# A list scheduler lays 600 plans, with a lag for TensorE's results, a rate for GpSimd beside VectorE, and one tile for two score banks

## The chip, the core and the metric

The kernel runs on one core of a Trainium2 chip. The metric is the device time of one execution in microseconds (us), the median of several runs. Besides, one execution is recorded by the hardware profiler; its span runs from the first to the last instruction of the core. The engines are called PE (TensorE's matmuls), PEld (its weight loads), DVE (VectorE), ACT (ScalarE), POOL (GpSimd) and SP (the queue that issues most DMAs). L918 is line 918 of the kernel before.

## What is computed

An attention with a block-causal mask (4 batches, 8 heads, 576 positions, head size 64) is followed by two MLPs over its 2304 tokens (512 to 2048 to 512), all in float32:

```python
scores = scale * q @ k.T                  # 8 heads, 4 batches, S = 576, D = 64
mask = pos[:, None] // 64 >= pos[None, :] // 64
attn = softmax(where(mask, scores, -1e9)) # exp, divided by sum + 1e-9
x = (attn @ v)                            # as (2304, 512)
r = maximum(x @ w_in, 0)                  # MLP 1
x = (s * (r * r) + b) @ w_out
h = x @ w2_in                             # MLP 2
return maximum(0.01 * h, h) @ w2_out
```

## The kernel before

**Tiles and stages.** Queries go in five blocks of 128 (the last of 64) positions, in the order 0, 1, 2, 4, 3 (`ORDER`). Block k sees 128 (k + 1) keys, the last one 576. MLP 1 of a block (`m_in`, `m_out`) runs while the attention of the next block is computed (`later_block`). MLP 1 has 16 hidden chunks f; each takes 4 chunks of three 512-column matmuls for h (L918; fp32r, split in a high and a low part, three products) and 4 times three for y (L961). ScalarE and VectorE make g, gh and gl from h between the two (L930 to L940). In the first block the weights of MLP 1 are decoded from pairs of words as they arrive (`first_weights`, `decode`, L345 to L371); from block 1 on the weights of MLP 2 are prepared and stored as `unit` (L461 to L495). After the last block, MLP 2 runs from 600 us on as seven products in place of eight over 384 columns (`in_pair`, L1174, and `out_phase`, L1239, with additions in L1154 and splits in L1046 and L1232).

**One attention unit** is a pair of heads of a batch. There are 16 for each block. The queries and keys are split (L712 to L716), TensorE writes the scores to the two banks `s` (L585 for blocks 0 and 1, L790 for the "flat" blocks 2 and 3, with two row groups in the array, L830 for block 4 with two halves of 288 keys), VectorE masks and takes the maximum (L796, L797, L834, L838), ScalarE the exponential with its sum (L800, L841), VectorE the reciprocal (L807, L848). Then p is normalised on GpSimd or VectorE (L577, L809, L849), TensorE transposes p by four 128-column pieces (L600) into bank `t`, ScalarE or VectorE takes that out as `pv` (L516, L518), and TensorE multiplies by v (L869).

**What sets the order.** All of this is put as steps into `Graph` by `G.add`: the engines that may do it with a cost on each, the steps whose result it needs (`after`), the buffers it opens and uses, a due time, whether it uses the port that VectorE and GpSimd share (`port`), the bytes of a DMA, the kind of TensorE work (`mode`: "f" for full matmuls, "r" for row-split scores, "c" for column-split products with v), and `behind`, steps that only must have been started before. `order` is an event-driven list scheduler: at each time every idle engine takes the ready step with the lowest due time whose buffers have room. On TensorE a change of mode counts as 10 times its `TURN` in due time. A result is there `LAT` = 0.04 us after a step's planned end. Of two steps with `port`, on VectorE and on GpSimd, one excludes the other. The steps are then issued in that order, each engine runs its own list in order, and real semaphores keep every dependency. In the plan, fillers (L622, dummy matmuls on `warm`) stand where TensorE has nothing else in the first 30 us.

The costs which the text uses: `act(n)` = 0.2 + n / 1200 us and 0.14 more with a sum, `dve(n)` = 0.155 + n / 960, `pool(n)` = 0.28 + 0.00085 n, a transpose 0.109, a chunk of three matmuls of T columns 3 (T / 2400 + 0.013).

## Time and profile before

| | us |
|---|---|
| median of 3 runs | 953.37 (953.12 to 954.3) |
| the profiled execution, device time | 956.59 |
| its span | 954.8 |
| TensorE's mean granted clock | 0.998 of full speed |

| engine | busy us | share | instructions |
|---|---|---|---|
| PE | 935.8 | 98% | 5780 |
| PEld | 828.2 | 87% | 5780 |
| DVE | 659.0 | 69% | 1321 |
| ACT | 564.7 | 59% | 1198 |
| POOL | 103.5 | 11% | 224 |

Busy is the time in which at least one instruction of the engine runs. A matmul's end is modelled and successive matmuls overlap, so TensorE's busy time tells where the engine had nothing at all, and not how fast it ran. Idle time is listed by the instruction that ended it and by what that one had waited for (the releaser).

### The profile page before, as it was taken

To read this page: it belongs to the slowest core of one execution; us is meant where nothing else is said; L and a number is where in the kernel's file an instruction comes from. 1 tells how busy PE (TensorE), PEld (TensorE's weight loads), DVE (VectorE), ACT (ScalarE), POOL (GpSimd) and SP (SyncE) were. 2 spreads that over 40 slices of the span, in tenths; PEclk is the share of its full clock that TensorE was granted. 3 is DMA by queue.
4 is the path that set the end of the run, shared out by engine and by line. 5 is a ranking of instruction groups with operands and counts; after the bars stand their busy time and mean duration, and the time that the engine had idled before them with its cause. 6 is when DMAs were issued, how large, how long until landed. Compare 5 with 4: busy or idle time off the path is not lost.

```text
span 954.8 us, 16614 instructions
## 1 busy us (share of the span) xinstructions
PE 935.8 (98%) x5780; PEld 828.2 (87%) x5780; DVE 659.0 (69%) x1321; ACT 564.7 (59%) x1198; POOL 103.5 (11%) x224
## 2 busy tenths in 40 slices
PE   9999999999999999999999999999999999999998
PEld 8677887777777888888878888899999999999998
DVE  5988878777587867766768664555595655855557
ACT  4766767675576656656558444454565646555443
POOL 1122221112121121122320000000000000000000
PEclk9999999999999999999999999999999999999999
DMA  8995487886748898587337981998229852147402
GB/s 235 341 303 184 130 290 222 287 308 181 231 136 262 262 303 260 153 251 233 110 94 236 383 284 60 372 417 363 98 61 330 309 183 100 50 181 292 162 1 67
DMA packets 147668, 208.27 MB, mean 218 GB/s; under 512 B 23552, under 2 KB 118400, under 8 KB 140928
## 3 DMA queue, kind: packets, MB, share of 16 engines
q1 hardware_dynamic: 145136, 206.42, 65.2%
q10 hardware_dynamic: 2448, 0.79, 0.4%
q8 instruction: 46, 0.75, 0.3%
q14 instruction: 38, 0.31, 0.1%
HBM read 154.47 MB, written 52.69 MB: 217 GB/s over the span
## 4 chain that ended last, share of the span: by engine, by line
PE 81%; DVE 6%; DMA 5%; ACT 2%; issue 2%; POOL 1%; SPq 1%; POOLq 0%; DVEq 0%; ACTq 0%
PE h L918 17%; PE y L961 16%; PE A L1239 10%; PE A L1174 10%; PE C L1174 5%; PE C L1239 5%; PE t L600 4%; PE o L869 4%; PE B L1239 3%; PE B L1174 2%; PE s L790 2%; PE s L585 1%; PE s L830 1%; PE warm L622 1%; DMA q<-in_q_dram 1%
## 5 line engine op out<-in xcount | busy, mean ns | idle before, releaser
L918 PE MATMUL h<-xh,w 128*128 128x512 f32 (+1 forms) x640 | 230.2, 389 | 2.2 <-DVE g L932 1.2
L961 PE MATMUL y<-gh,w 128*128 128x512 f32 (+1 forms) x640 | 185.8, 374 | 0.9 <-ACT yo L516 0.9
L918 PEld LDWEIGHTS h<-xh,w 128*128 128x128 f32 x640 | 119.2, 190 | 29.7 <-issue 4.1
L961 PEld LDWEIGHTS y<-gh,w 128*128 128x128 f32 x640 | 114.3, 188 | 21.2 <-ACT yo L516 1.2
L1232 ACT ACTIVATE gh<-G 128x384 fp32r<-128x384 f32 x168 | 86.9, 525 | 57.0 <-PE A L1239 21.6
L918 PE MATMUL h<-xl,w 128*128 128x512 f32 (+1 forms) x320 | 118.9, 372 | 0.7 <-DVE xl L698 0.7
L961 PE MATMUL y<-gl,w 128*128 128x512 f32 (+1 forms) x320 | 118.4, 370 | 0.0
L1174 PE MATMUL A<-xh,wi 128*128 128x384 f32 x384 | 112.9, 337 | 1.0 <-DVE G L1154 0.9
L1046 DVE TENSOR_TENSOR gl<-G,gh 128x384 fp32r<-128x384 f32 x168 | 91.4, 554 | 30.4 <-ACT gh L1232 28.7
L1239 PE MATMUL A<-gh,wo 128*128 128x384 f32 x384 | 98.0, 336 | 1.4 <-DVE Y L1154 1.4
L934 ACT ACTIVATE g<-h 128x512 f32<-128x512 f32 (+1 forms) x80 | 44.2, 553 | 84.1 <-PE h L918 77.2
L600 PE MATMUL t<-id_sb,p 128*128 128x128 f32 x400 | 67.5, 280 | 6.6 <-POOL p L577 3.1
L1174 PEld LDWEIGHTS A<-xh,wi 128*128 128x128 f32 x384 | 70.6, 188 | 2.9 <-DVE G L1154 1.5
L1239 PEld LDWEIGHTS A<-gh,wo 128*128 128x128 f32 x384 | 69.1, 188 | 2.4 <-DVE Y L1154 2.3
L961 PEld LDWEIGHTS y<-gl,w 128*128 128x128 f32 x320 | 60.3, 188 | 10.9 <-DVE gl L937 0.5
L600 PEld LDWEIGHTS t<-id_sb,p 128*128 128x128 f32 x400 | 46.8, 141 | 26.0 <-POOL p L577 5.9
L918 PEld LDWEIGHTS h<-xl,w 128*128 128x128 f32 x320 | 60.9, 190 | 8.2 <-DVE xl L698 1.0
L1188 ACT ACTIVATE G<-G 128x384 f32<-128x384 f32 x72 | 37.6, 524 | 47.2 <-DVE G L1154 47.2
L937 DVE TENSOR_TENSOR gl<-g,gh 128x512 fp32r<-128x512 f32 (+1 forms) x80 | 50.8, 635 | 20.1 <-ACT gh L936 16.5
L1174 PE MATMUL A<-xl,wi 128*128 128x384 f32 x192 | 64.5, 336 | 0.0
L1239 PE MATMUL A<-gl,wo 128*128 128x384 f32 x192 | 64.2, 335 | 0.0
L1046 DVE TENSOR_TENSOR G<-G 128x384 f32<-128x384 f32 x96 | 53.2, 555 | 12.8 <-ACT G L1188 11.2
(125 smaller groups left out, 1834.5 us busy)
## 6 DMA issues: line engine op xcount, KB each, us to landing
wi<-u_in SPq DMA_DIRECT2D x32, 896.0 KB, 7.8
wo<-u_out SPq DMA_DIRECT2D x28, 1024.0 KB, 9.0
w<-kept SPq DMA_DIRECT2D x16, 1024.0 KB, 7.9
u_in<-unit SPq DMA_DIRECT2D x16, 896.0 KB, 5.9
u_out<-unit SPq DMA_DIRECT2D x32, 448.0 KB, 4.6
early<-in_moe_w_in_dram SPq DMA_DIRECT2D x16, 512.0 KB, 5.9
early<-in_moe_w_out_dram SPq DMA_DIRECT2D x16, 512.0 KB, 6.4
kept<-w SPq DMA_DIRECT2D x8, 1024.0 KB, 7.7
```

The costliest lines, as they stand in the source:

```text
L600: e.transpose(tb()[:, x * 128:(x + 1) * 128], P()[:, pc:pc + 128], id_sb)
L790: e.matmul(out=o[h][:, :nk], lhsT=qs()[r, qc], rhs=kk()[r, :nk], start=(n == 0), stop=(n == 2))
L869: e.matmul(out=o()[64 * h:64 * h + 64, n * x:n * x + n], lhsT=V()[:, j, 64 * h:64 * h + 64], rhs=r, start=(j == 0), stop=(j == nj - 1),)
L918: e.matmul(out=h()[:, :T], lhsT=w()[:, wi, c * 128:(c + 1) * 128], rhs=x[blk, c]()[:, :T], start=(c == 0 and n == 0), stop=(c == KD - 1 an ...
L934: a = G.add({"ACT": act(T)}, lambda e: e.activation(out=g()[:, :T], in_=h()[:, :T], func=ACTF.Relu), [prev], [g], [h], due)
L937: lo = G.add({"DVE": dve(T)}, lambda e: e.tensor_tensor(out=gl()[:, :T], in0=g()[:, :T], in1=gh()[:, :T].bitcast(F32), op=ALU.subtract), [ ...
L961: e.matmul(out=y()[:, :W], lhsT=w()[:, wi, d * 128:(d + 1) * 128], rhs=x()[:, :W], start=(pos == 0 and n == 0), stop=(pos == NF - 1 and n ...
L1046: e.tensor_tensor(out=out, in0=x, in1=y, op=ALU.subtract)
L1174: e.matmul(out=x()[:, :NH], lhsT=in_w[n, i, c]()[:, s, ai], rhs=y()[:, c], start=(first and c == 0 and m == 0), stop=(c == 1 and m == 2), ...
L1188: {"ACT": act(NH)}, lambda e, y=y: e.activation(out=y(), in_=y(), func=ACTF.Lrelu), [a], [], [y], d2 + 2)
L1232: hi = G.add({"ACT": act(NH)}, lambda e, gh=gh, x=x: e.activation(out=gh(), in_=x(), func=ACTF.Copy), [a], [gh], [x], due - 2)
L1239: e.matmul(out=z[d]()[:, :NH], lhsT=out_w[n, r]()[:, 2 * i + d, s], rhs=y(), start=(first and i == 0 and m == 0), stop=(i == 3 and m == 2) ...
```

## The change

`order` becomes a search around the scheduler, which is now called `plan`. It lays the plan once with the due times as written, and then 599 times with some of them moved: it draws a stretch of 5, 15, 40 or 100 us of the best plan so far, moves the due times of 30% of the steps in it by up to 1.5 us either way, and for steps that may run on two engines sometimes fixes one. A plan that ends no later than the best becomes the best. The random numbers have a fixed seed. In `plan`:

- A result of TensorE is there `DRAIN` later (0.14, 0.25 or 0.32 us by mode).
- Steps with `port` on VectorE and GpSimd no longer exclude each other. While a VectorE step with `port` runs, a GpSimd step proceeds at 1 − `HELD` = 40% of its rate; VectorE is not slowed.
- Chunks of one sum on TensorE, and the parts of one unit's scores, are chained by `behind` in place of `after`; the products with v and the four parts of a product in `out_phase` are chained too.
- Each buffer gets its slot from the plan (`slot`), in the order in which slots came free, in place of a count.
- The two score banks are one tile of [128, 2, 512]. In the flat blocks, one memset and one maximum cover both heads; the block of 576 keys has one step on TensorE for both halves, one maximum over both, one exponential with one sum, and no minimum and sum of two halves.
- The loads of v for block 1 stay free of a wait; the products with v of block 0 now count in `att_done`.

`EARLY` is not used. The diff, cut to its core:

```diff
+    PLANS = 600
+    DRAIN = {"f": 0.14, "r": 0.25, "c": 0.32}
+    HELD = 0.6
+    EARLY = 13.7
...
     def order(self):
+
+        kept = [(s.left, s.due, s.eng) for s in self.steps]
+        users = {b: b.users for s in self.steps for b in s.uses}
+        for i, s in enumerate(self.steps):
+            s.place = (s.due, i)
+        r = random.Random(1)
+        best, moved, at, out = None, [(0.0, None)] * len(kept), None, None
+        for _ in range(self.PLANS):
+            new = list(moved)
+            if best is not None:
+                a, w = r.uniform(0.0, best), r.choice((5, 15, 40, 100))
+                for i, x in enumerate(at):
+                    if a <= x < a + w and r.random() < 0.3:
+                        d, e = new[i]
+                        if len(kept[i][2]) > 1 and r.random() < 0.5:
+                            e = r.choice([None, *kept[i][2]])
+                        new[i] = d + r.uniform(-1.5, 1.5), e
+            for s, (left, due, eng), (d, e) in zip(self.steps, kept, new):
+                s.left, s.due, s.at = left, due + d, None
+                s.eng = eng if e is None else {e: eng[e]}
+            for b, u in users.items():
+                b.users = u
+            got = self.plan()
+            if best is None or got is not None and self.end <= best:
+                best, moved, at = self.end, new, [s.at for s in self.steps]
+                out = [(s, s.on, s.at, s.eng) for s in got], {b: b.slot for b in users}
+        for s, *x in out[0]:
+            s.on, s.at, s.eng = x
+        for b, x in out[1].items():
+            b.slot = x
+        self.end = best
+        return [x[0] for x in out[0]]
+
+    def plan(self):
...
-            turn[k].sort(key=lambda s: s.rank, reverse=True)
+            turn[k].sort(key=lambda s: s.place, reverse=True)
...
+                    room[s.key] += 1
+                    slots[s.key].append(s.slot)
...
-                    if port is s:
-                        port = None
+                elif what == "pool":
+                    if e == turn_no:
+                        idle["POOL"], busy = True, None
+                        heapq.heappush(events, (t + self.AGAIN["POOL"], n, "done", s, None))
+                        n += 1
...
+                    b.slot = slots[b.key].pop(0)
...
-                if s.port and e in ("DVE", "POOL"):
-                    port = s
...
+                if e in ("DVE", "POOL") and s.port:
+                    if e == "POOL":
+                        busy = [s, s.eng[e] - self.AGAIN[e], t]
+                    elif busy is not None:
+                        u = min(max(held, busy[2]), t)
+                        busy[1:] = busy[1] - (1 - self.HELD) * (u - busy[2]) - (t - u), t
+                    if e == "DVE":
+                        held = end
+                    if busy is not None:
+                        w = max(held - t, 0.0)
+                        left = busy[1]
+                        left = left / (1 - self.HELD) if left <= w * (1 - self.HELD) else left + w * self.HELD
+                        turn_no += 1
+                        heapq.heappush(events, (t + left, n, "pool", busy[0], turn_no))
+                        n += 1
+                    if e == "POOL":
+                        continue
...
+                if e == "PE":
+                    end += self.DRAIN[s.mode]
...
+        "h": (ps("ps_h", 1), 1), "s": (ps("ps_s", 1), 2), "t": (ps("ps_t", 1), 1),
...
+            x = b.slot * ptn if name == "pt" else npt * ptn + b.slot * vn
...
+        if key == "s":
+            b = Buf("s", lambda: s_both()[:, b.slot])
+            return b
...
+        a = G.add({"PE": 0.208 * 4}, av, [*tr, fv_ok, pads], [o], [pt, fv] + [spare] * (p > 1), due, mode="c", behind=att_done if att_done[0] else [])
+        att_done[0] = a
...
+            vl = [G.add({"SP": 0.65}, v_load, before if blk > 1 else [], fresh, [V4], due=due - 8, run=512, nbytes=512 * (nk // 128 * 128))]
...
-                            e.matmul(out=o[h][:, :nk], lhsT=qs()[r, qc], rhs=kk()[r, :nk], start=(n == 0), stop=(n == 2))
+                            e.matmul(out=s_both()[:, h, :nk], lhsT=qs()[r, qc], rhs=kk()[r, :nk], start=(n == 0), stop=(n == 2))
...
-                    mk = G.add({"DVE": 0.13}, lambda e, x=bk[h]: e.memset(x()[:64, nk - 64:nk], NEG), [sc], uses=[bk[h]], due=due - 4.5)
-                    mx.append(G.add({"DVE": dve(nk)}, lambda e, nm=nm, h=h, x=bk[h]: e.reduce_max(out=nm()[:, h:h + 1], in_=x()[:, :nk], axis=AX.X, negate=True),
-                                    [mk], [nm] * (h == 0), [nm, bk[h]], due=due - 4))
+                mk = G.add({"DVE": dve(128)}, lambda e: e.memset(s_both()[:64, :, nk - 64:nk], NEG), [sc], uses=bk, due=due - 4.5)
+                mx = [G.add({"DVE": dve(2 * nk)}, lambda e, nm=nm: e.reduce_max(out=nm()[:, 0:2], in_=s_both()[:, :, :nk], axis=AX.X, negate=True),
+                            [mk], [nm], [nm, *bk], due=due - 4)]
...
-                    sc.append(G.add({"PE": 3 * (half / 2400 + 0.013)}, fn, ok, [bk[j]], [kh, kl_, qs], due - 5))
+                            e.matmul(out=s_both()[:, j, :half], lhsT=qs()[:, qc, :128], rhs=kk()[:, half * j:half * j + half], start=(n == 0), stop=(n == 2))
+
+                sc = G.add({"PE": 6 * (half / 2400 + 0.013)}, fn, ok, bk, [qs, kh, kl_], due - 5)
...
-                neg = G.add({"DVE": 0.2}, lambda e, nm=nm: e.tensor_scalar(
-                    out=nm()[:, 0:1], in0=nm()[:, 0:1], scalar1=nm()[:, 1:2], scalar2=None, op0=ALU.min), mx, uses=[nm], due=due - 4)
-                ex = [
...
+                mx = G.add({"DVE": dve(nk)}, lambda e, nm=nm: e.reduce_max(out=nm()[:, 0:1], in_=s_both()[:, :, :half], axis=AX.XY, negate=True),
+                           [sc], [nm], [nm, *bk], due=due - 4)
+                ex = G.add({"ACT": act(nk, 1, True)}, lambda e, nm=nm, l=l, P=P: e.activation(
+                    out=P()[:, :nk].rearrange("p (j n) -> p j n", j=2), in_=s_both()[:, :, :half], func=ACTF.Exp, bias=nm()[:, 0:1], scale=1.0,
+                    accum_out=l()[:, 0:1]), [mx], [l], [P, l, nm, *bk], due - 3.5)
+                a = G.add({"DVE": 0.17}, lambda e, l=l: e.tensor_scalar(
+                    out=l()[:, 0:1], in0=l()[:, 0:1], scalar1=1e-9, scalar2=None, op0=ALU.add), [ex], uses=[l], due=due - 3)
...
+            a = G.add({"PE": many * nj * 0.206 * n / 128}, av, [x for c in pair for x in c[3]], [o] + [xf] * (pair[0][0] == 0), [xf, *[x for c in pair for x in (c[2], c[4])]], due, mode="c", behind=[last_av])
+            last_av = a
...
-                {"PE": 3 * (T / 2400 + 0.013)}, fn, [prev, w_ok[blk, f, 0], *x_ok[blk, c]], [h] * (c == 0),
-                [h, w, xh_t[blk, c], xl_t[blk, c]], due + c * 0.01,
+                {"PE": 3 * (T / 2400 + 0.013)}, fn, [w_ok[blk, f, 0], *x_ok[blk, c]], [h] * (c == 0),
+                [h, w, xh_t[blk, c], xl_t[blk, c]], due + c * 0.01, behind=[prev] * (c > 0),
...
-                {"PE": 3 * (T / 2400 + 0.013)}, fn, [hi, lo, w_ok[blk, f, 1], y_last.get((blk, d))],
-                [y] * (pos == 0), [y, w, gh, gl], due + d * 0.01,
+                {"PE": 3 * (T / 2400 + 0.013)}, fn, [hi, lo, w_ok[blk, f, 1]],
+                [y] * (pos == 0), [y, w, gh, gl], due + d * 0.01, behind=[y_last[blk, d]] if pos else [],
...
-                p = G.add({"PE": ONE}, fn, after, z if first and i == 0 else [], [*z, gh, gl, out_w[n, r]], due)
+                p = G.add({"PE": ONE}, fn, after, z if first and i == 0 else [], [*z, gh, gl, out_w[n, r]], due, behind=[p] if i else [])
```

## Rows read from the trace of the kernel before

**Rows 1.** Page, first part: busy us (share of the span), instructions.

```profile
PE 935.8 (98%) x5780; PEld 828.2 (87%) x5780; DVE 659.0 (69%) x1321; ACT 564.7 (59%) x1198; POOL 103.5 (11%) x224
```

**Rows 2.** By stretch: length, busy (instructions) PE, PEld, DVE, ACT, POOL; PEclk, DMA, GB/s.

```profile
0.00:30.00 30.00, 28.33 (x204) 25.36 (x204) 18.64 (x41) 15.75 (x73) 4.75 (x18) 1.00 0.92 255
30.00:80.00 50.00, 45.94 (x243) 35.84 (x243) 46.56 (x82) 36.97 (x69) 12.45 (x24) 1.00 0.92 304
80.00:520.00 440.00, 432.78 (x2983) 354.85 (x2984) 324.20 (x723) 285.08 (x622) 86.27 (x183) 1.00 0.70 216
...
600.00:950.00 350.00, 347.66 (x1989) 344.59 (x1988) 220.07 (x414) 188.64 (x380) 0.00 (x0) 1.00 0.54 200
```

**Rows 3.** TensorE's waits: who for whom, total us, times, longest us.

```profile
PE t L600 <- POOL p L577: 3.1, 3, 1.6
PE t L600 <- POOL p L809: 2.6, 4, 1.7
PE A L1239 <- DVE Y L1154: 1.4, 3, 0.5
PE warm L622 <- POOL wq L512: 1.3, 1, 1.3
PE h L918 <- DVE g L932: 1.2, 2, 1.1
PE y L961 <- ACT yo L516: 0.9, 1, 0.9
PE o L869 <- DVE pv L518: 0.9, 1, 0.9
PE A L1174 <- DVE G L1154: 0.9, 2, 0.7
PE h L918 <- DVE xl L698: 0.7, 1, 0.7
```

**Rows 4.** Timeline at 237 us: start, length, instruction, [idle before, releaser].

```profile
236.02 2.91 POOL L809 TENSOR_SCALAR p<-p,l 128x384 f32<-128x384 f32 x2 [5.18 <-DVE l L807]
...
236.26 2.22 DVE L485 TENSOR_TENSOR unit<-unit 128x1792 f32<-128x1792 f32 x1 [0.43 <-ACT unit L484]
...
238.99 0.55 PE L600 MATMUL t<-id_sb,p 128*128 128x128 f32 x3 [1.68 <-POOL p L809]
...
239.57 0.60 ACT L516 ACTIVATE pv<-t 128x512 f32<-128x512 f32 x1 [1.83 <-PE t L600]
```

**Rows 5.** By stretch, just behind it, columns as in rows 2.

```profile
239.00:241.00 2.00, 2.00 (x12) 1.55 (x13) 0.67 (x3) 1.43 (x4) 0.00 (x0) 0.81 0.96 283
241.00:243.00 2.00, 2.00 (x6) 1.52 (x6) 2.00 (x4) 1.29 (x4) 0.00 (x0) 0.50 0.95 284
```

**Rows 6.** Line L485, VectorE's 1792-column subtraction: ns shortest, median, longest.

```profile
L485 DVE TENSOR_TENSOR unit<-unit x16: 2015/2024/2223, 152.7 to 595.1; 128x1792 f32<-128x1792 f32 x16
```

**Rows 7.** GpSimd by line and shape: busy us, mean ns, idle before.

```profile
L809 POOL TENSOR_SCALAR p<-p,l 128x384 f32<-128x384 f32 x32 | 22.1, 703 | 83.7 <-DVE l L807 58.2 <-PE h L918 12.7 <-DVE s L796 7.7
...
L577 POOL TENSOR_SCALAR p<-p,l 128x192 f32<-128x192 f32 x16 | 13.8, 862 | 60.4 <-DVE l L564 46.1 <-ACT p L555 6.0 <-ACT w L368 4.9
```

**Rows 8.** Line L809, flat blocks' normalisation: ns shortest, median, longest.

```profile
L809 POOL TENSOR_SCALAR p<-p,l x63: 577/691/2348, 163.5 to 500.1; 128x384 f32<-128x384 f32 x32, 128x512 f32<-128x512 f32 x31
```

**Rows 9.** VectorE by line and shape: maxima and minimum of the scores.

```profile
L797 DVE TENSOR_REDUCE nm<-s 128x1 f32<-128x512 f32 x32 | 21.1, 683 | 0.0
...
L834 DVE TENSOR_REDUCE nm<-s 128x1 f32<-128x288 f32 x32 | 13.8, 450 | 1.1 <-PE s L830 1.0
...
L838 DVE TENSOR_SCALAR nm<-nm 128x1 f32<-128x1 f32 x16 | 3.3, 205 | 0.0
```

**Rows 10.** Timeline at 426 us: weight loads around row-split scores.

```profile
426.13 0.19 PEld L790 LDWEIGHTS s<-kh,qs 64*128 64x128 f32 x2 [0.17 <-issue]
...
427.02 0.19 PEld L918 LDWEIGHTS h<-xh,w 128*128 128x128 f32 x1 [0.36 <-issue]
```

**Rows 11.** Page, DMA issues: count, KB each, us to landing.

```profile
w<-kept SPq DMA_DIRECT2D x16, 1024.0 KB, 7.9
```

More of the change, by code (lines that the diff above doesn't have):

```diff
@@ L1 @@
 import heapq
+import random
+from bisect import insort
 from contextlib import ExitStack
@@ L27, in __init__ @@
     def __init__(self, key, make):
-        self.key, self.make, self.users, self.t, self.opener = key, make, 0, None, None
+        self.key, self.make, self.users, self.t, self.opener, self.slot = key, make, 0, None, None, None
     def __call__(self):
@@ L91, in order @@
     def order(self):
+        kept = [(s.left, s.due, s.eng) for s in self.steps]
[30 more added lines that the diff above has]
+    def plan(self):
         room = dict(self.room)
+        slots = {k: list(range(n)) for k, n in room.items()}
         idle = {e: True for s in self.steps for e in s.eng}
@@ L95, in order @@
         events, n, out_there = [], 0, 0
-        port, dma, mode = None, 0.0, "f"
+        dma, mode, busy, held, turn_no = 0.0, "f", None, 0.0, 0
         out = []
@@ L100, in order @@
             s.rank = (s.due, i)
+            s.need = {}
+            for b in s.opens:
+                s.need[b.key] = s.need.get(b.key, 0) + 1
+            s.need = list(s.need.items())
             for b in s.opens:
@@ L126, in order @@
                         if not b.users:
-                            heapq.heappush(events, (t + self.LAT, n, "room", b.key, None))
+                            heapq.heappush(events, (t + self.LAT, n, "room", b, None))
                             n += 1
@@ L180, in order @@
                     out_there += 1
+                if e == "PE":
+                    end += self.DRAIN[s.mode]
                 heapq.heappush(events, (end, n, "done", s, e))
                 n += 1
-        left = [s for s in self.steps if s.at is None]
-        assert not left, (len(left), [s.fn.__qualname__ for s in left[:5]])
         self.end = t
-        return out
+        return None if any(s.at is None for s in self.steps) else out
 def act(n, ptr=0, acc=False):
@@ L286, in __call__ @@
             return self.view(self.buf())
-    pv_t, taken = [], {}
+    pv_t = []
     def slot(k, name):
@@ L587, in scores @@
             fresh.add(bk)
-            out.append(G.add({"PE": max(n * 1.67e-3, 0.214) - 0.06}, fn, after, new, [bk, *q, *kk], due - 5))
+            out.append(G.add({"PE": max(n * 1.67e-3, 0.214) - 0.06}, fn, after, new, [bk, *q, *kk], due - 5, behind=out[-1:]))
         return out
@@ L727, in later_block @@
         before = [att_done[0]]
+        last_av = att_done[0]
         V4 = None
@@ L785, in fn @@
                 def fn(e, qs=qs, kh=kh, kl=kl_, bk=bk):
-                    o = [x() for x in bk]
+                    for x in bk:
+                        x()
                     for n, (qc, kk) in enumerate(((0, kh), (0, kl), (1, kh))):
@@ L825, in later_block, with fn @@
                 kh, kl_, qs, ok = score_parts(Q, K, nk, ql, kl, due)
-                sc = []
-                for j in range(2):
-                    def fn(e, j=j, bk=bk, kh=kh, kl=kl_, qs=qs):
+                def fn(e, bk=bk, kh=kh, kl=kl_, qs=qs):
+                    for x in bk:
+                        x()
+                    for j in range(2):
                         for n, (qc, kk) in enumerate(((0, kh), (0, kl), (1, kh))):
-                            e.matmul(out=bk[j]()[:, :half], lhsT=qs()[:, qc], rhs=kk()[:, half * j:half * j + half], start=(n == 0), stop=(n == 2))
-                    sc.append(G.add({"PE": 3 * (half / 2400 + 0.013)}, fn, ok, [bk[j]], [kh, kl_, qs], due - 5))
+                            e.matmul(out=s_both()[:, j, :half], lhsT=qs()[:, qc, :128], rhs=kk()[:, half * j:half * j + half], start=(n == 0), stop=(n == 2))
@@ L832, in later_block @@
+                sc = G.add({"PE": 6 * (half / 2400 + 0.013)}, fn, ok, bk, [qs, kh, kl_], due - 5)
                 nm, l = buf("sm", [128, 8], F32, "nm"), buf("sm", [128, 8], F32, "l")
-                mx = [
-                    G.add({"DVE": dve(half)}, lambda e, j=j, bk=bk, nm=nm: e.reduce_max(out=nm()[:, j:j + 1], in_=bk[j]()[:, :half], axis=AX.X, negate=True),
-                          [sc[j]], [nm] * (j == 0), [nm, bk[j]], due - 4)
-                    for j in range(2)
-                ]
```

62 lines of the change are left out of this document (28 added, 34 removed).

## The prediction

> **What bounds the kernel now.** I read the page's first part, then a table by stage, then TensorE's list of waits, and only then single stretches. The page has TensorE at 935.8 of 954.8 us [rows 1], so the time is TensorE's instruction stream plus its holes. The holes: 30.00 − 28.33 = 1.7 us before 30 us, 50.00 − 45.94 = 4.1 us from 30 to 80, 440.00 − 432.78 = 7.2 us from 80 to 520, 350.00 − 347.66 = 2.3 us from 600 to 950 [rows 2]. Of 954.8 − 935.8 = 19.0 us that leaves 3.7 us, nearly all in the last 4.8 us, where the last additions and stores run after the last matmul and no order helps. By cause [rows 3]: transposes that wait for GpSimd's normalisation of p, 3.1 + 2.6 = 5.7 us in 7 waits; evacuations in MLP 1 and at its start, 1.2, 0.9, 0.9 and 0.7 us; additions of G and Y in MLP 2, 0.9 and 1.4 us; one fixed wait of 1.3 us for the first memset. A hole has a second price: after the one of 1.68 us that ends at 238.99, the granted clock is 0.81 for 2 us and then 0.50, the 1.2 GHz level, for 2 us [rows 4, 5]: 2 × 0.19 + 2 × 0.50 = 1.4 us are lost that show as busy time.
>
> The change takes no matmul and no DMA away. It lays the work out in another order, so it can win the holes, their clock price and what turning between kinds of TensorE work costs; it can lose by opening new holes, since every engine runs its list in order.
>
> **The change part by part.** The profiled execution took 956.59 us with a span of 954.8, so 1.8 us lie around the span, and it was 3.2 us above the median of 953.37. Gains are counted in that span and taken off the median.
>
> (a) *GpSimd's rate.* In the plan of before, a GpSimd step and a VectorE step on the shared port exclude each other. The trace says otherwise. Two normalisations of 384 columns start at 236.02 and take 2.91 us; VectorE's 1792-column subtraction starts beside them at 236.26 and takes 2.22 us [rows 4], where 16 such subtractions have a median of 2.02 and 2.22 as the longest [rows 6]. So VectorE loses 0.2 us and GpSimd pays. The same shows in the mean of 862 ns for 192 columns, above the 703 ns for 384 [rows 7]: the small ones stand beside the weight decoding. The new planner lets VectorE run on and slows GpSimd to 40% meanwhile. That is the right direction: it will put TensorE's transposes later, behind other matmuls. Bounds: none of the 5.7 us of holes and 1.4 us of clock, or all 7.1. I take 5, nearer the upper end, because the holes are few and single, and the matmuls of MLP 1 around them have no wait but those listed.
>
> Is 40% right? The pair had 0.24 us before the subtraction began and 0.45 us after its end at 238.48. The shortest normalisation takes 577 ns [rows 8], so the pair is 1.16 us of work, and 1.16 − 0.69 = 0.47 us of it went through in 2.22 us: 21%. With the mean of 703 ns it is 0.72 of 2.22, 32%. The plan is still too hopeful, by 2.22 × 0.19 = 0.42 us for such a meeting (0.18 at 32%).
>
> The Trainium skill (SBUF — State Buffer, section "SBUF: two separate sides") goes further: the shared ports are an exclusive lock which the first comer keeps for its whole instruction, while the other is blocked fully. The trace follows it only in part: by it the subtraction would have waited 0.34 us for the first normalisation and the second would have ended 0.58 us behind it; they show 0.2 and 0.45. What such a lock would do here is a rival below.
>
> (b) *Lag of TensorE's results.* Three transposes start at 238.99. At the 0.109 us each that the planner gives them they are done at 239.32, but ScalarE, idle for 1.83 us until them, starts at 239.57 [rows 4]. The lag is 0.25 us; the old plan has 0.04, the new one 0.04 + 0.14. It bears on the waits for g, yo, pv and the additions of G and Y, 1.2 + 0.9 + 0.9 + 0.9 + 1.4 = 5.3 us [rows 3], the upper bound; the lower is 0. In MLP 1 TensorE can choose between attention and MLP, so I take 1.5 of 3.0; in MLP 2 a bank must be emptied before its next use, so 0.5 of 2.3. Together 2.
>
> (c) *Chains as order instead of as results* (`behind`). The next chunk of a sum is ready 0.01 us after the start of the one before, not 0.04 us after its end, so the chunks of one h come back to back and h reaches ScalarE earlier, which is within the 2 of (b). On TensorE the same matmuls run in another order: 0. Cover: TensorE has other work for 98% of the time [rows 1]. The chains now forced on the scores, the attention products and the second product of MLP 2 take freedom away; at worst one of them stops TensorE like one wait for Y, 0.5 us, the longest of its three [rows 3]. I take 0.
>
> (d) *One tile for two score banks.* For 576 keys, two maxima of 450 ns and a minimum of 205 become one maximum over 576 elements; 450 ns for 288 and 683 for 512 [rows 9] are 1.04 ns an element and 0.15 fixed, so 0.75 us, and 0.90 + 0.21 − 0.75 = 0.36 us less for each of 16 units. For the 32 units with 384 and 512 keys one fixed share goes in the maxima and at most one in the memsets: 0.3. Together at most 16 × 0.36 + 32 × 0.3 = 15 us of VectorE, which is at 324.20 of 440 us where these stand [rows 2]. In the time: 0, covered by TensorE; where TensorE does wait for p, each wait is shorter by up to 0.36. Against it, both banks now come free only after both halves of the exponential, and the 576-key scores start only when both are free: for 16 units the scores may come half an exponential later, 0.3 us by the planner's costs, behind MLP matmuls. Net 0, bounds −1 to +1.
>
> (e) *Six hundred layouts.* A draw moves due times by up to 1.5 us in a stretch of 5 to 100 us and stays if the plan ends no later. Beyond the holes it can win turns: around one group of row-split scores the weight loader stood 0.17 and 0.36 us [rows 10]. There are 32 such groups, 32 × 0.53 = 17 us if all could go; but a group must be entered and left, unless two become neighbours. Bounds 0 and a fifth of it, 3.4; I take 1, nearer to none, as the row shows both ends of a single group. The DMAs move too, on SP's queue, where they issue in order: the DMA engines are at 0.92 up to 80 us and 0.70 after [rows 2]. A kept weight lands in 7.9 us [rows 11] and is due 30 us ahead, so 0, at worst 1.
>
> (f) *The start.* Up to 80 us there are 5.8 us of holes, of which 1.3 is fixed and part is GpSimd's, in (a). VectorE is at 46.56 of 50.00 us from 30 to 80 [rows 2], so little is to be had: 0 to 3, I take 1.
>
> (g) *What the tighter plan loses.* Filling holes moves steps closer to the results that they need, and GpSimd is still taken as too fast. There are 112 normalisations (two for each of 48 units, one for each of 16). If 5 of them stop TensorE by 0.42, it is 2 us. Bounds 0 to 8 (20 of them); I take 2, as before had 7 such waits.
>
> Sum: 5 + 2 + 0 + 0 + 1 + 1 − 2 = 7 us, and 953.4 − 7 = **946.4 us**.
>
> **The rivals.**
>
> *Hidden anyway.* Every hole that is filled opens one elsewhere, because VectorE is the next bound: it is loaded to 93% from 30 to 80 us and to 74% from 80 to 520 [rows 2]. For it: the first stage. Against: 74% leaves room, and the listed holes are single events. Time 953.4, within 1.9.
>
> *The plan trusts GpSimd too far (slower).* Place: transposes from 30 to 520 us. With the exclusion gone, the plan puts normalisations beside VectorE's long steps as a rule, and each may cost TensorE 0.42 us. It decides where the 9 us of gains are used up: (9 + 1.9) / 0.42 = 26 of 112 in which TensorE stands right behind one. With 33, 14 us: 953.4 − 9 + 14 = 958. For it: the pair at 236 us. Against: the plan before put transposes too early with no such account at all, and had 7 waits [rows 3].
>
> *GpSimd stands still meanwhile.* The same with no progress beside VectorE: 2.22 − 0.6 × 2.22 = 0.89 us for a meeting, 13 decide, and 20 give 953.4 − 9 + 18 = 962. The row has 21 to 32% of progress, so this is unlikely. It is what the Trainium skill's page SBUF — State Buffer, in the section named above, would make of it.
>
> *It doesn't do what it says.* The search lowers the end of the planner's model, and nearly half the draws fall into the last 435 us, which TensorE fills; if nothing of (e) and (f) comes, 953.4 − 5 = 948, inside the forecast.
>
> *Far better.* All of (a), (b), (e), (f): 7.1 + 5.3 + 3.4 + 3 = 19 us, 934.
>
> **How the numbers follow.** A measurement of this kernel tells about 0.2% (1.9 us) from no change. Forecast (2 to 15 us won) 0.60; far better 0.08; hidden 0.15; trusts too far 0.13; stands still 0.04. So faster 0.68, same 0.15, slower 0.17. Range 938 to 957: out are the 0.08 below, the 0.04, and half of the 0.13 above.
>
> **What the profile after would show.** (a) right: the transposes' waits for GpSimd fall from 5.7 to under 2 us, and no stretch at 1.2 GHz is left in the middle; wrong: more such waits, behind longer normalisations. (b): waits for g, yo and pv shorter. (c): h chunks in runs of 12 matmuls. (d): VectorE's busy time 5 to 15 us less. (e): TensorE's busy time from 80 to 520 us shrinks by more than the clock's 1.4. The prediction is wrong if the time to 80 us or MLP 2 moves by more than 2 us, since both are held at nearly nothing.

## The result: 963.5 us, 1% slower, and the profile after

The changed kernel takes 963.48 us (median of 4 runs, 962.25 to 963.68) against 953.30 us for the kernel before beside it (953.12 to 954.3): a ratio of 1.0103, 95% interval 1.0088 to 1.0118. 946.4 us was forecast, and the range ended at 957. The profiled execution took 963.68 us, its span is 961.9.

The page's first part answers to [rows 1]. TensorE is still at 98%, but for 2.7 us longer; VectorE does 64 fewer instructions and is busy for 4.7 us more, where the prediction looked for 5 to 15 us less; GpSimd has 44 fewer:

```profile
PE 938.5 (98%) x5780; PEld 826.7 (86%) x5780; DVE 663.7 (69%) x1257; ACT 568.6 (59%) x1178; POOL 89.3 (9%) x180
```

The table by stretch answers to [rows 2] (length, busy us of PE, PEld, DVE, ACT, POOL, then PEclk, DMA, GB/s):

```profile
0.00:30.00 30.00, 28.23 (x198) 25.40 (x200) 16.90 (x38) 14.84 (x67) 4.75 (x18) 1.00 0.88 257
30.00:80.00 50.00, 46.10 (x247) 36.46 (x244) 45.85 (x83) 37.43 (x73) 12.76 (x20) 0.97 0.86 287
80.00:520.00 440.00, 434.93 (x3014) 358.06 (x3013) 335.50 (x665) 290.26 (x605) 71.75 (x142) 1.00 0.71 220
...
600.00:950.00 350.00, 342.37 (x1931) 333.45 (x1930) 210.81 (x398) 182.46 (x371) 0.00 (x0) 1.00 0.51 190
```

From 80 to 520 us the holes shrink from 7.2 to 5.1 us and 31 more matmuls are started (3014 against 2983). TensorE's busy time there is 2.2 us longer and not shorter, so the sign named for (e) did not come; with 31 more matmuls in the stretch that says little. From 600 to 950 us the holes grow from 2.3 to 7.6 us and 58 fewer are started. TensorE's waits, which answer to [rows 3], say at what:

```profile
PE s L1251 <- ACT G L1226: 3.5, 6, 0.6
PE A L1251 <- DVE G L1231: 2.8, 6, 0.8
PE t L680 <- ACT early L431: 2.6, 1, 2.6
PE t L680 <- POOL p L657: 2.4, 5, 0.9
PE s L873 <- ACT p L635: 1.5, 1, 1.5
```

L1251 is the first product of MLP 2 (L1174 before), L1226 and L1231 are the evacuations of its banks on ScalarE and VectorE. The list of before had 0.9 us of a first product's waits for VectorE (L1154) and none for ScalarE (L1149). The transposes wait 2.4 us for L657 (L577 before), and 0.3 us for the block of 576 keys; the flat blocks' normalisation (2.6 us before) has left the list.

MLP 1 ends with its last accumulation on y. By the rows of that line (shortest, median, longest ns, then first and last start), for before and after:

```profile
L961 PE MATMUL y<-gl,w x320: 276/389/500, 42.3 to 600.0; 128*128 128x512 f32 x128, 128*128 128x258 f32 x32
```

```profile
L1038 PE MATMUL y<-gl,w x320: 279/389/446, 46.2 to 593.7; 128*128 128x512 f32 x128, 128*128 128x258 f32 x32
```

So the part up to there became 6.3 us shorter, and the rest of the span went from 954.8 − 600.0 = 354.8 us to 961.9 − 593.7 = 368.2 us, 13.4 us longer. That is the whole loss, and more.

**Why MLP 2 waits.** The timeline of the changed kernel at 670 us (start, length, instruction, [idle before, releaser]):

```profile
670.50 0.34 PE L1251 MATMUL s<-xh,wi 128*128 128x384 f32 x1
...
671.37 0.51 PE L1251 MATMUL s<-xh,wi 128*128 128x384 f32 x2
...
672.41 0.34 PE L1251 MATMUL s<-xh,wi 128*128 128x384 f32 x1
672.78 0.49 ACT L1226 ACTIVATE G<-s 128x384 f32<-128x384 f32 x1 [3.68 <-PE s L1251]
...
673.33 0.44 PE L1251 MATMUL s<-xh,wi 128*128 128x384 f32 x1 [0.58 <-ACT G L1226]
...
674.74 1.02 DVE L1231 TENSOR_TENSOR G<-s,G 128x384 f32<-128x384 f32 x2 [5.79 <-PE s L1251]
```

Six matmuls fill one half of the tile `s` from 670.50, six the other half from 671.54 on (the second of the pair at 671.37 is the first of these). The first half is full at about 671.7, and ScalarE, idle since 669.10, could take it out then. It starts at 672.78, just behind the last matmul *on the other half*. The third group goes on the first half again, must wait until that is out, and starts at 673.33: 0.92 us after the start before it, where 0.17 is the usual distance, so 0.75 us are lost. The list shows only 0.58 of it, since a matmul's modelled end lies 0.17 us beyond the start of its successor. Counted by start-to-start distances, MLP 2's matmuls stand 0.1 us or more beyond their 0.1735 us in 59 places, 15.5 us together; before it was 15 places and 4.3 us.

That a bank and its neighbour wait for each other is no need of the chip. The Trainium skill (PSUM — Partial Sum Buffer, section "PSUM bank collisions raise a hardware error") asks for a guard by bank, or more finely by bank and group of 32 partitions, and not across banks; the run e3 below agrees, where ScalarE takes out one bank while TensorE fills the other. It is the program: an access to one half of the tile `s`, which lies over two banks, is ordered here against accesses to its other half too.

This does not hold for every tile. In before the two maxima of a flat unit write two columns of one tile `nm`, and each exponential reads its own. The first exponential stands behind both maxima in the plan, and still it starts ahead of the second one:

```profile
161.03 0.58 ACT L800 ACTIVATE p<-s,nm 128x384 f32<-128x384 f32 x1
161.46 0.54 DVE L797 TENSOR_REDUCE nm<-s 128x1 f32<-128x384 f32 x1
```

### The profile page after: what moved, and what is told of

It reads as the page before. It is cut to its first block, busy times and chain, and to the rows that moved or that the text cites. A ratio compares the mean times of both kernels' runs of the same rounds, so it can differ in the third digit from the quotient of the medians.

```text
span 961.9 us, 16488 instructions
## 1 busy us (share of the span) xinstructions
PE 938.5 (98%) x5780; PEld 826.7 (86%) x5780; DVE 663.7 (69%) x1257; ACT 568.6 (59%) x1178; POOL 89.3 (9%) x180
## 3 DMA queue, kind: packets, MB, share of 16 engines
q1 hardware_dynamic: 145136, 206.42, 64.5%
## 4 chain that ended last, share of the span: by engine, by line
PE 82%; DVE 6%; ACT 4%; DMA 4%; issue 2%; SPq 1%; POOL 1%; DVEq 0%; ACTq 0%; POOLq 0%
PE y L1038 17%; PE h L995 15%; PE A L1316 10%; PE A L1251 9%; PE s L1251 8%; PE C L1316 5%; PE t L680 4%; PE o L945 4%; PE s L995 3%; PE s L1316 3%; PE s L873 2%; DMA fk<-in_k_dram 1%; PE s L913 1%; DVE G L1231 1%; DMA early<-in_moe_w_out_dram 1%
## 5 line engine op out<-in xcount | busy, mean ns | idle before, releaser
L1038 PE MATMUL y<-gh,w 128*128 128x512 f32 (+1 forms) x640 | 190.1, 380 | 0.1
L995 PE MATMUL h<-xh,w 128*128 128x512 f32 (+1 forms) x552 | 183.2, 382 | 0.3
L1038 PEld LDWEIGHTS y<-gh,w 128*128 128x128 f32 x640 | 111.8, 189 | 20.2 <-issue 2.1
L995 PEld LDWEIGHTS h<-xh,w 128*128 128x128 f32 x552 | 102.0, 189 | 22.9 <-issue 2.8
L1251 PE MATMUL A<-xh,wi 128*128 128x384 f32 x384 | 112.8, 339 | 3.3 <-DVE G L1231 2.8
L995 PE MATMUL h<-xl,w 128*128 128x512 f32 (+1 forms) x276 | 101.6, 368 | 0.2 <-DVE xl L779 0.2
L1251 PE MATMUL s<-xh,wi 128*128 128x384 f32 x288 | 85.0, 341 | 4.5 <-ACT G L1226 3.5
L1231 DVE TENSOR_TENSOR G<-s,G 128x384 f32<-128x384 f32 x48 | 26.2, 555 | 76.5 <-PE s L1251 56.8
L1251 PEld LDWEIGHTS A<-xh,wi 128*128 128x128 f32 x384 | 70.6, 188 | 7.4 <-DVE G L1231 5.3
L680 PE MATMUL t<-id_sb,p 128*128 128x128 f32 x384 | 62.5, 276 | 5.5 <-ACT early L431 2.6
L1011 ACT ACTIVATE g<-h 128x512 f32<-128x512 f32 (+1 forms) x69 | 37.8, 548 | 46.5 <-PE h L995 45.5
L1251 PE MATMUL A<-xl,wi 128*128 128x384 f32 x192 | 64.4, 335 | 0.0
```

The source lines that it names most:

```text
L680: e.transpose(tb()[:, x * 128:(x + 1) * 128], P()[:, pc:pc + 128], id_sb)
L995: e.matmul(out=h()[:, :T], lhsT=w()[:, wi, c * 128:(c + 1) * 128], rhs=x[blk, c]()[:, :T], start=(c == 0 and n == 0), stop=(c == KD - 1 an ...
L1011: a = G.add({"ACT": act(T)}, lambda e: e.activation(out=g()[:, :T], in_=h()[:, :T], func=ACTF.Relu), [prev], [g], [h], due)
L1038: e.matmul(out=y()[:, :W], lhsT=w()[:, wi, d * 128:(d + 1) * 128], rhs=x()[:, :W], start=(pos == 0 and n == 0), stop=(pos == NF - 1 and n ...
L1231: e.tensor_tensor(out=out, in0=in_, in1=out, op=ALU.add)
L1251: e.matmul(out=x()[:, :NH], lhsT=in_w[n, i, c]()[:, s, ai], rhs=y()[:, c], start=(first and c == 0 and m == 0), stop=(c == 1 and m == 2), ...
```

## The experiments

The diffs are cut to their core. Two theories at first. *A, the tile*: MLP 2 loses because the two banks are one tile. *B, the plan*: the search closes MLP 2 up beyond what the chip follows. Then the planner's parts, one by one, on two tiles.

**e1, two tiles again.** The planner as changed; two tiles, and the steps on them separate as before.

```diff
-            s_t.append(pools["s"][0].tile([128, 2, 512], F32, tag="s", name="s"))
+            s_t.extend(pools["s"][0].tile([128, 512], F32, tag=f"s{x}", name=f"s{x}") for x in range(2))
```

> The changed kernel's planner (search, results' lag, GpSimd's rate, chains) with the two score banks as two tiles again and the steps on them separate, as in the kernel before. Theory A (the one tile makes each bank wait for the other, and this costs 13 us in MLP 2 and up to 5 us before its first matmul in MLP 1): 945 to 949 us, MLP 2 (last matmul on L1038's accumulators to the end) back to 355 us. Theory B (the search's own order loses it: MLP 2 laid out tighter than the chip can follow): 960 us or more, MLP 2 still 365 us or more.

941.65 us, ratio to before 0.9879 (0.9864 to 0.9893). From MLP 1's last start (586.7) to the end of the span (939.5) it takes 352.8 us. In MLP 2 no wait is left; the list for the whole kernel is this:

```profile
PE t L680 <- POOL p L657: 2.9, 6, 1.1
PE t L680 <- DVE p L650: 2.0, 1, 2.0
PE warm L702 <- POOL wq L592: 1.3, 1, 1.3
PE y L1044 <- DVE yo L600: 0.5, 1, 0.5
PE t L680 <- ACT early L431: 0.3, 1, 0.3
```

Theory A's number, and 3 us better. B is out as the only cause, but the plan is another one here; e3 holds it fixed.

**e2, one tile in the kernel before.** Plan and order of every engine are those of before; the two banks are the halves of one tile.

```diff
+        return s_t[0][:, (s_n[0] - 1) % 2]
...
+        if key == "s":
+            return Buf("s", s_bank)
```

> The kernel before, its plan and every engine's order unchanged; only the two score banks are halves of one tile (no step merged). Theory A: slower than before by 8 to 20 us (961 to 973 us), most of it in MLP 2, with PE waiting on the DVE and ACT evacuations of the other bank. Theory B: 953 us, within 2 us of before.

969.53 us, ratio 1.0173 (1.0156 to 1.019). The size is A's, the place is not: MLP 1's last start moves from 600.0 to 611.2, and from there to the end it is 356.1 us, only 1.3 more than before. The loss is in the attention. ScalarE's idle time ahead of the flat blocks' exponentials, by what ended it (us, times), in before and in e2:

```profile
  DVE nm L797: 2.2, 4
```

```profile
  DVE nm L807: 15.1, 21
```

With separate steps on one tile, the first head's exponential waits for the second head's maximum as well, though both only read `s`: in before it starts ahead of that maximum's end in 20 of the 32 flat units, in e2 in none. That TensorE's 11.2 us come from this wait is likely and not shown.

**e3, the same order, two tiles from the last block's MLP on.** Every engine's list is that of the changed kernel. Where the last block first needs a bank for h (498 us), the tile is given up and two are opened in its place. In the traces no matmul (fillers aside) and no instruction of VectorE, ScalarE or GpSimd has changed its place.

```diff
-            b = Buf("s", lambda: s_both()[:, b.slot])
+            b = Buf("s", lambda: s_one(b.slot) if one else s_both()[:, b.slot])
...
-        A, B, C = bank("h" if i % 2 == 0 else "t", "A"), bank("s", "B"), bank("s", "C")
+        A, B, C = bank("h" if i % 2 == 0 else "t", "A"), bank("s", "B", True), bank("s", "C", True)
```

> The changed kernel with the same plan and the same order on every engine; from the last block's first-layer banks on (some 498 us) the one tile is given up and the two banks are two tiles. Theory A: MLP 2 falls from 368 to about 355 us, the whole to about 950 us, the start unchanged (first MLP matmul at 35 us). Theory B: no change, 962 to 964 us.

946.36 us, ratio 0.9924 (0.9909 to 0.9939), 17.1 us less than the changed kernel. MLP 1's last start to the end: 944.4 − 590.5 = 353.9 us, so 14.3 of the spans' 17.5 us are MLP 2's. Of the other 3.2 us, 1.7 are the clock in the start of the changed kernel's profiled execution (below), and 1.3 a first score matmul at 8.48 us in place of 7.20; up to there the two programs are the same. The same matmuls as in the timeline above, now 4.3 us earlier:

```profile
667.39 0.34 PE L1266 MATMUL s<-xl,wi 128*128 128x384 f32 x1
667.42 0.49 ACT L1241 ACTIVATE G<-s 128x384 f32<-128x384 f32 x1 [2.63 <-PE s L1266]
667.57 0.51 PE L1266 MATMUL s<-xh,wi 128*128 128x384 f32 x2
...
668.09 0.51 PE L1266 MATMUL s<-xh,wi 128*128 128x384 f32 x2
668.43 0.34 PE L1266 MATMUL s<-xl,wi 128*128 128x384 f32 x1
668.53 0.56 DVE L1246 TENSOR_TENSOR G<-s,G 128x384 f32<-128x384 f32 x1 [3.94 <-PE s L1266]
```

The first half is taken out at 667.42 beside the second group, and the third group follows with no hole. Of the 59 places 2 are left, with 0.7 us. That settles A for MLP 2. Why e2 lost so little there is not shown by a run of its own. In the order of before a group on another bank (A) nearly always stands between two groups on `s`, so that the neighbour can be out by the time it is waited for: in e2's list two first-product groups on different `s` banks adjoin in 2 places, in the changed kernel's in 17. The planner may close them up since its model takes the banks as independent; with one layout (e10) it is 10 places, so the search does a part of it.

**e4, two tiles in blocks 0 and 1 as well.** The same order; the one tile stands only in blocks 2 to 4.

```diff
-        o = bank("s", "o")
+        o = bank("s", "o", True)
```

> As the run before, and block 0 and block 1 work on two tiles as well; the one tile stands only in blocks 2 to 4, where the merged steps are. Same plan and order. Theory A: first MLP matmul back near 30 us and the whole at about 945 us. If the start's 5 us come from the plan and not from the tile, the same as the run before (950 us). Theory B: 962 to 964 us.

944.04 us, ratio 0.9901 (0.9887 to 0.9916). 2.3 us less than e3. Of the 2.1 us between the two spans 1.0 lie in MLP 2 (352.9 against 353.9 us), where both have two tiles, so some 1 to 2 us are the tile's in blocks 0 and 1. The first MLP matmul stands at 34.2 us, not 30: the late start is the plan's. VectorE is busy for 663.3 us here and for 676.7 in e1. The steps that were merged (memsets, maxima, the minimum and the sum of two halves) take 54.5 us here and 67.6 in e1, 13.1 less, and e1 without that saving is 2.4 us faster.

**e5, one layout** in place of 600, otherwise e1.

```diff
-    PLANS = 600
+    PLANS = 1
```

> The run with two tiles, and one layout instead of 600: the planner's new costs without the search. If the search is worth little (the prediction's step on the layouts gave it 1 us): 942 to 944 us. If the search is where most of the 12 us come from: 949 us or more.

957.09 us, ratio to before 1.0028 (1.0014 to 1.0042). The new costs and chains alone gain nothing; the search gains 15.4 us on them. (These are differences of medians. By the ratios to the kernel before, measured beside each run, the differences to e1 are somewhat smaller: 14.2 us for e5, 5.9 for e6, 3.0 for e8, 13.3 for e9, 6.1 for e12.) Of e5's waits the longest stand at the start of MLP 2 and behind VectorE in the start:

```profile
PE A L1257 <- ACT G L1232: 3.9, 2, 3.0
PE t L680 <- DVE p L650: 2.0, 1, 2.0
```

**e6, no lag of TensorE's results** in the plan, otherwise e1.

```diff
-    DRAIN = {"f": 0.14, "r": 0.25, "c": 0.32}
+    DRAIN = {"f": 0.0, "r": 0.0, "c": 0.0}
```

> The run with two tiles, 600 layouts, and the lag of TensorE's results set to nothing in the plan. The prediction gave the lag 2 us: 943 to 945 us, with PE's waits for evacuations in MLP 2 somewhat longer. If the lag is where most of the gain comes from: 948 us or more. If the search finds its way without it: 941 to 942 us.

948.35 us, ratio 0.9941 (0.9925 to 0.9957): under the search the lag is worth 6.7 us, three times the step's 2. Against the expectation PE waits for nothing in MLP 2; it loses from 300 to 500 us, where e1 loses 13.0 us and e6 18.2 (worked out as for the table below).

**e7, another seed**, otherwise e1: `random.Random(2)` in place of `random.Random(1)`.

> The run with two tiles, the search's random numbers started from another seed: how much of a difference is the draw. 940 to 944 us if the plans of one search are as good as another's; if it differs by over 3 us, smaller differences between the other plans say nothing about their causes.

940.91 us, ratio 0.9868 (0.984 to 0.9896), the same within the interval. The draw itself moves the time little, as far as two seeds can tell; each run below stands on one draw.

**e8, VectorE and GpSimd exclude each other** in the plan as before, otherwise e1.

```diff
...
+                    if s.port and e in ("DVE", "POOL") and port is not None or s.nbytes and out_there >= self.LANES:
...
```

> The run with two tiles, 600 layouts, and the rule of the kernel before for VectorE and GpSimd (in the plan, neither starts a port step while the other has one). The prediction gave the new rate 5 us: 945 to 948 us, and PE waiting on GpSimd's normalizing in the middle as before, 5 us or so. If the rate has no part in it: 941 to 943 us.

944.90 us, ratio 0.991 (0.9888 to 0.9931). 3.3 us more than e1, with intervals that overlap slightly. The transposes wait 3.4 us for GpSimd (2.9 in e1), not 5. GpSimd has 213 instructions here and 178 in e1: with the rate the plan gives more of the work to VectorE. Of the 120 normalising instructions GpSimd does 100 here, 65 in e1 and 69 in e5, which has the rate and no search.

**e9, the search on the costs of before**: e8 without the lag. The new chains and the two tiles stay.

> Two tiles, 600 layouts, and the costs of the kernel before in the plan (VectorE and GpSimd exclude each other, no lag): the search without the new costs. If the search alone carries the 12 us: 941 to 944 us. If the new costs are worth under the search what their single removals showed (3 and 7 us): 948 to 953 us.

956.27 us, ratio 1.0019 (1.0009 to 1.0028), 3 us beyond the worse expectation. With a plan that doesn't know of the two effects, 600 layouts win nothing on the chip, and the old waits stay:

```profile
PE t L662 <- POOL p L873: 3.0, 4, 1.3
PE t L662 <- POOL p L639: 2.1, 3, 1.0
```

**e10, the changed kernel with one layout**, one tile and all.

> The changed kernel, one tile and all, with one layout instead of 600. If the one tile costs MLP 2 its 14 us in any order of the new planner: 14 us more from MLP 1's last matmul to the end than the two tiles with one layout (which took 361.3 us), some 375 us. If it costs that only in an order that the search has closed up so far that each bank's evacuation is counted on at once: 361 to 364 us, and the whole within 4 us of 957 us.

962.77 us (957.74 to 964.12), ratio 1.0078 (1.005 to 1.0105). From MLP 1's last start to the end 962.3 − 602.0 = 360.3 us, against 361.3 for e5; the whole is 5.7 us above e5, not 4, though one of its four runs took 957.74. The total of MLP 2 fits the second expectation, but it doesn't tell the two apart: e5 loses 7.5 us in the first 100 us of MLP 2 and 1.0 after (table below), e10 1.4 and 6.6. What one tile costs in an order without search is open; what it costs in one order is known from e2 (1.3 us) and e3 (14.3 us).

**e11, 1500 layouts** in place of 600, otherwise e1.

> Two tiles, 1500 layouts instead of 600, same seed. If the search still has something to find that the chip follows: 937 to 940 us. If its model is the limit by now: 940 to 943 us.

939.04 us (938.61 to 940.69), ratio 0.9842 (0.9827 to 0.9856), the fastest of all, though e7's interval takes it in. It beats both kernels, by 15 and by 24 us.

**e12, the chains of before** (`after` in place of `behind`; none on the scores, the attention's products and `out_phase`), otherwise e1. Nothing holds the four parts of a product of `out_phase` in order here, and the search puts one part behind its sums' evacuation: on the banks A the trace has one product taken out after 18 of its 24 matmuls, and 30 ahead of the next. So two of the sums of MLP 2 lack a part; the matmuls are the same in number.

```diff
-                {"PE": 3 * (T / 2400 + 0.013)}, fn, [w_ok[blk, f, 0], *x_ok[blk, c]], [h] * (c == 0),
+                {"PE": 3 * (T / 2400 + 0.013)}, fn, [prev, w_ok[blk, f, 0], *x_ok[blk, c]], [h] * (c == 0),
...
-                p = G.add({"PE": ONE}, fn, after, z if first and i == 0 else [], [*z, gh, gl, out_w[n, r]], due, behind=[p] if i else [])
+                p = G.add({"PE": ONE}, fn, after, z if first and i == 0 else [], [*z, gh, gl, out_w[n, r]], due)
```

> Two tiles, 600 layouts, lag kept, and the chains of the kernel before: a chunk of a sum counts as waiting for the end and the lag of the chunk before it, and no chains on scores, attention products and MLP 2's second product. The prediction gave the new chains 0: 940 to 943 us. If the lag needs them (the plan would put 0.14 us and more between chunks): 946 us or more.

948.86 us, ratio 0.9943 (0.9928 to 0.9958), 7.2 us more than e1: the second expectation. The chains together are worth that beside a lag; which of them, the run doesn't tell. The search can't do without the one in `out_phase` for the sum's sake.

**Where each kernel loses its time.** Worked out from the traces: a time less the work that TensorE had started by then, where each matmul counts with the shortest usual distance to its successor (173.5 ns for 384 columns, 226.5 for 512, fillers nothing). The whole work is 879.1 us in every kernel. Us lost up to the time in the heading:

| | 60 | 300 | 500 | 600 | 700 | 930 |
|---|---|---|---|---|---|---|
| before | 23.9 | 46.8 | 64.9 | 66.8 | 70.1 | 71.4 |
| after | 28.2 | 46.6 | 60.6 | 63.3 | 66.6 | 78.5 |
| e3, same order, late banks two tiles | 25.5 | 44.2 | 58.8 | 59.6 | 60.0 | 61.2 |
| e1, two tiles | 25.5 | 42.5 | 55.5 | 55.8 | 56.0 | 56.1 |
| e2, before with one tile | 26.2 | 50.6 | 74.3 | 77.7 | 81.2 | 83.9 |
| e5, one layout | 25.8 | 42.4 | 62.2 | 63.6 | 71.1 | 72.1 |
| e9, search on the old costs | 24.2 | 43.5 | 62.4 | 64.5 | 65.9 | 69.9 |
| e10, one tile, one layout | 27.8 | 50.4 | 67.7 | 70.9 | 72.3 | 78.9 |

The search on the new costs (e1 against e5) wins most between 300 and 500 us, 19.8 − 13.0 = 6.8 us, and at the entry of MLP 2, 7.5 − 0.2 = 7.3 us.

## Why the prediction was wrong

The sign was decided by step (d), the one tile, which was sized at 0 with bounds of −1 to +1. With plan and order held, it costs 963.48 − 946.36 = 17.1 us from the last block on by the medians; of that the table has (78.5 − 60.6) − (61.2 − 58.8) = 15.5 us from 500 us on, and the rest lies ahead of it, where both run the same program. With 1 to 2 us in blocks 0 and 1 the tile costs some 17 to 19 us. The mechanism is that each half of the tile waits for accesses to the other, and the step put that at nothing. The step looked at the planner's account (both banks are opened and freed together in the attention) and at VectorE's instructions. It never asked who else calls `bank("s")`: the last block's h, the banks B and C of every first product of MLP 2, and B of the second. Nor what an access to half of a tile waits for. No row of before could show that, since there each bank was a tile; so the row to bound it by was MLP 2's own evacuation wait, 0.9 us in two places [rows 3], times the pairs that use B and C. The half of the step on VectorE was right: at most 15 us less, 13.1 measured (e4 against e1), and no gain in time to be seen from it. VectorE's whole busy time rose all the same, by 4.7 us, for a reason that belongs to (a).

Without the tile's waits the sum would have come out near: e4, in the same order and with one tile in blocks 2 to 4 alone, is 9.5 us faster than before, and 7 were forecast. That is luck, since most of the terms below were wrong one by one.

The sign to watch was named ("wrong if the time to 80 us or MLP 2 moves by more than 2 us") and came: MLP 2 moved by 13.4.

(e), the search: 1 us forecast from the turns of row-split scores. It is worth 15.4 us on the new costs (e5 to e1), and on the old ones it gains nothing against before (e9, 956.3). The step took the search for a small gain of its own; it is what turns the costs of (a) to (c) into time.

(a), (b), (c): 5, 2 and 0 were forecast, as gains of the costs themselves. Alone they gain nothing (e5). Under the search their removals cost 3.3 us (e8), 6.7 (e6) and 7.2 us (e12), which don't add, since e9 without the first two loses 14.6. Direction right for (a) and (b): the transposes' waits for GpSimd fell from 5.7 us [rows 3] to 2.4 + 0.3, not under the 2 named; the waits for yo and pv are gone and the one for g fell from 1.2 to 0.7 us; and between 60 and 520 us no stretch of 4 us is below 0.97 of the full clock, where before had one of 0.57 at 240. (c)'s 0 was mis-sized: the step said that TensorE has other work anyway, but e12 fits a chain that decides what the plan believes of the lag. Its sign, runs of 12 matmuls on h, came in part: 26 of them, where before had 4.

(a)'s reading of the trace was wrong. The row at 236 us [rows 4] merges two normalisations. In windows that part the two, the first took 0.59 us, its usual time, and the second, begun beside the subtraction, 2.35:

```profile
236.02 0.59 POOL L809 TENSOR_SCALAR p<-p,l 128x384 f32<-128x384 f32 x1 [5.18 <-DVE l L807]
236.26 2.22 DVE L485 TENSOR_TENSOR unit<-unit 128x1792 f32<-128x1792 f32 x1 [0.43 <-ACT unit L484]
236.58 2.35 POOL L809 TENSOR_SCALAR p<-p,l 128x384 f32<-128x384 f32 x1
```

From the subtraction's end at 238.48 the second needed 0.45 us more, 0.13 less than the 0.58 of the shortest one. So in 1.90 us beside VectorE it got on by 0.13 us. A short meeting says the same:

```profile
430.29 0.42 DVE L937 TENSOR_TENSOR gl<-g,gh 128x256 fp32r<-128x256 f32 x1
430.43 0.85 POOL L809 TENSOR_SCALAR p<-p,l 128x512 f32<-128x512 f32 x1 [7.06 <-DVE l L807]
```

VectorE ends at 430.71, and GpSimd 0.56 us later, 0.13 less than the 0.69 of the shortest 512 columns. In before, after, e1, e8 and e9 there are 23 normalisations that began while one TENSOR_TENSOR or SCALAR_TENSOR_TENSOR on SBUF tiles ran and met nothing else of VectorE: each got on by 0.12 to 0.14 us, whether 0.2 or 1.9 us of VectorE's instruction were left. So the rate is neither 40% nor 21 to 32%: beside such a step GpSimd stands still, but for that start. Nor did the gain come by transposes put later, as (a) had it: the rate makes the plan move normalisations to VectorE, 53 of 120 in place of 9, 26.3 us in place of 5.3. For the flat blocks, where before had 63 on GpSimd [rows 8] and 1 on VectorE, the changed kernel has:

```profile
L890 POOL TENSOR_SCALAR p<-p,l x35: 588/749/2193, 160.6 to 491.5; 128x384 f32<-128x384 f32 x19, 128x512 f32<-128x512 f32 x16
L890 DVE TENSOR_SCALAR p<-p,l x29: 402/479/926, 160.8 to 499.2; 128x512 f32<-128x512 f32 x16, 128x384 f32<-128x384 f32 x13
```

The 21.0 us that come to VectorE by this are more than the 13.1 that the merged steps save.

(f), the start: 1 us was to be won, 4.3 were lost by 60 us (table). Of these 1.1 are a later first score matmul (8.48 us against 7.41 in before), which is no part of the change, as e3 with the same program up to there has it at 7.20. Four transposes of block 0 wait 2.58 us with the fillers used up:

```profile
33.37 0.41 DVE L650 TENSOR_TENSOR p<-p,l 128x256 f32<-128x256 f32 x1
...
33.94 0.83 PE L680 MATMUL t<-id_sb,p 128*128 128x128 f32 x4 [2.58 <-ACT early L431]
```

The profile names ScalarE's decoding; VectorE's normalisation, queued behind a decoding step and a split, ends at 33.78, just ahead of the transposes. Behind the hole the granted clock falls (0.55 and 0.59 of full speed from 34 to 38 us, near the 1.2 GHz level, 2 × 0.45 + 2 × 0.41 = 1.7 us lost; e3, with the same hole and the same order, stays at 1.00):

```profile
34.00:36.00 2.00, 2.00 (x10) 1.90 (x11) 1.33 (x3) 1.16 (x2) 0.00 (x0) 0.55 0.99 381
36.00:38.00 2.00, 2.00 (x8) 1.25 (x8) 2.00 (x3) 0.48 (x1) 0.00 (x0) 0.59 0.25 92
```

In e3 the hole ends at 32.66 us, and the rows behind it are:

```profile
32.00:34.00 2.00, 1.34 (x10) 1.31 (x11) 1.96 (x5) 1.30 (x3) 0.00 (x0) 1.00 1.05 283
34.00:36.00 2.00, 2.00 (x21) 1.42 (x19) 2.00 (x3) 0.85 (x2) 0.00 (x0) 1.00 0.94 316
```

With two tiles in blocks 0 and 1 (e1, e4, e5) a wait of 2.0 to 2.6 us is still there, so it is the plan's; by 60 us it costs e1 25.5 − 23.9 = 1.6 us against before.

(g), what the tighter plan loses: 2 us at GpSimd were forecast. The tighter order did lose, but at the banks that the plan took for independent.

The rivals: none of them named the tile, so the range's upper end stood for another mechanism. "Trusts GpSimd too far" and "stands still" asked for longer waits of the transposes; the waits became shorter, with 53 normalisations on VectorE. Yet the premise of "stands still" was right, as the 23 meetings show. It is the exclusive lock of the Trainium skill (SBUF — State Buffer, section "SBUF: two separate sides"), and the trace agrees with it for GpSimd as the second to start, but for those 0.13 us; the prediction found it followed only in part, from the merged row. "Far better", 934 us, with a chance of 0.08, is what the planner comes near to without the tile: 941.65, and 939.04 with 1500 layouts. "Doesn't do what it says" failed for the search.

## What to carry to other kernels

Before two PSUM banks are put into one tile, list everything that uses either, over the whole kernel, and ask of each pair whether one half must wait for the other; a step saved on an engine with room is worth less than one such wait in a stretch where TensorE never pauses. A schedule search gives what its model knows: here it won nothing with the old costs and 12 us with better ones, though one of these, GpSimd's rate, was itself wrong; and it put groups on the two halves of the tile side by side, counting on an independence that the tile had taken away. So put every wait that the program really has into the model ahead of the search, and hold the order fixed (as e3 does) to price a wait. And read a merged row singly before a rate is worked out from it.

## What the runs showed of the hardware

TensorE's listed waits understate holes between pipelined matmuls: at 673 us 0.58 us was listed and 0.75 lost, and over MLP 2 the list has 6.5 us where the start-to-start distances have 15.5. And after the same hole of 2.58 us, in the same order, the granted clock fell in one profiled execution (0.55 and 0.59 for 4 us) and not in another (1.00): one such hole may or may not cost the clock. Last, a GpSimd normalisation begun beside a TENSOR_TENSOR or SCALAR_TENSOR_TENSOR of VectorE on SBUF tiles got on by 0.12 to 0.14 us until that instruction's end, in all 23 such meetings.
